# A fused attention and spectral-mixing kernel: two more quad loads, the last two modes by column halves, identity passes moved

## The chip, the cores and the metric

The kernel runs on one core of a Trainium2 chip. The metric is device time in microseconds (us) of one execution. The runs of the kernel before took 427.29, 425.5 and 425.84 us; the median is 425.84 us. One further execution was profiled: it took 425.88 us.

## The reference

Two stages are chained. The first is a sparse causal attention on 8 batches, 8 heads, 576 positions and head size 64. Heads 0 to 3 see the last 32 positions ("local"), heads 4 to 7 see every 32nd earlier position ("strided"). The second takes the heads side by side as `x` (8 x 576 x 512) and mixes it in the frequency domain:

```python
X = np.fft.rfft(x, axis=1)
Xr, Xi = (np.real(X[:, :n_modes]), np.imag(X[:, :n_modes]))
Yr = np.einsum('bmd,mde->bme', Xr, w_r) - np.einsum('bmd,mde->bme', Xi, w_i)
Yi = np.einsum('bmd,mde->bme', Xr, w_i) + np.einsum('bmd,mde->bme', Xi, w_r)
Y[:, :n_modes] = Yr + 1j * Yi
y = np.fft.irfft(Y, n=S, axis=1)
u = x + y
return (u + np.maximum(u @ w_ch, 0.0)).astype(np.float32)
```

There are 64 modes, and each has its own pair of 512 x 512 weights. In float32 these are 134 MB of the inputs, while q, k and v are 9.4 MB each and the output is 9.4 MB.

## The kernel before, in words

All loads that change float32 to float16 are issued by GpSimd (POOL), in program order: q, k, v by batch, then the mode weights. The weights are taken in "halves": half 1 holds input rows 256 to 511 of each mode and half 0 holds rows 0 to 255. `ORDER` lists (half, mode): modes 0 to 55 of half 1, 0 to 47 of half 0, then the 8 last of half 1 and the 16 last of half 0. Two consecutive entries are a "pair". A pair is loaded by two DMAs, one of `moe_w_r` into partitions 0 to 63 and one of `moe_w_i` into partitions 64 to 127, of 512 KB (float16) each. At the pair numbers in `QUADS` two pairs are loaded together by two DMAs of 1024 KB.

`w_fetch` (the function that issues at lines 187 to 194) is called after each consumed pair. It counts a free pair and issues while there is room: a pair needs one free pair, a quad needs two, and it returns without issuing when there are fewer. The weights live in `wring`, a ring of five pairs; pairs 1, 2 and 7 are guests in other buffers, and consuming them frees nothing. Eight pairs (0 to 7) are issued during the strided attention. The local attention of batch b then runs on TensorE (PE) in a hand-written order, mixed with `NMODES[b]` modes, 14 for batch 0, so pairs 0 to 6 are consumed in batch 0. `load_loc(6)` is issued just before them and `load_loc(7)` at the start of batch 1. All waits between engines follow from which tiles the instructions touch. Where a matmul and another engine use one PSUM bank, they take turns even on different columns.

After half 1's 56 and half 0's 48 modes, 24 modes remain (`rest`, line 1073). Half 0 is computed one mode at a time by `mode` (lines 619 to 652): 4 column blocks `e` of 128, 4 contraction steps each, 16 matmuls (L634) into one PSUM bank that holds eight modes. VectorE (DVE) then adds the half-1 part from PSUM and writes the spectrum `YT` (`spectrum`, L567): once for modes 56 to 61, once for 62 and 63. Between the modes `late[i]` inserts other work: `renew` updates `x` and `x @ w_ch` by the first 48 modes (L966, L769, L971), and after mode 62 it starts output items 0 and 1: `v_early(0)`, `v_early(1)`, `u_early(0)`. These are identity matmuls of 128 x 512 that copy `x @ w_ch` (L997) or `x` (L1007) into PSUM.

When mode 63 is done, `spec_z(3, 0)` (L745) multiplies batches 0 to 3 of the last spectrum by `w_ch`; ScalarE (ACT) copies it to `zzs[0]`; eight transposes (L1076) give the spectrum itself, copied by DVE (L1078) to `yys`. These two tiles lie in a PSUM pool of their own, opened when the pool of the modes is closed.

The output has 18 items, each of two 128 x 512 blocks. An item needs `v_early` and `new_rows` on `zzs` (L1018) in one PSUM pair, a relu by ACT (L1041, float32), `u_early` and `new_rows` on `yys` in another PSUM pair, a DVE add (L1055) and a store issued by SyncE (SP, L1058). `pieces(k)` says whether the add and the store go by whole item or by halves. `pooled(k, j)` says whether GpSimd adds `x` to the relu's result (L1044) in place of an identity matmul.

Of the kernel before, what the change touches and what calls it, by code (L numbers as in the profile page):

```python
# [10 lines left out]
FP = mybir.dt.float32  # L11
F16 = mybir.dt.float16
AluOp = mybir.AluOpType
ACTF = mybir.ActivationFunctionType
# [5 lines left out]
NM = 64  # L20
# [36 lines left out]
def kernel(  # L57
# [10 lines left out]
    nc = tc.nc  # L68
    PSUM = bass.MemoryType.PSUM
# [5 lines left out]
    pss = {}  # L75
# [10 lines left out]
    def psum(kind, half=False, pair=False):  # L86
        if pair:
            return pss[kind].tile([128, 2, 512], FP, tag=kind, name=kind)
        if half:
            return pss[kind].tile([128, 1024], F16, tag=kind, name=kind)  # L90
        return pss[kind].tile([128, 512], FP, tag=kind, name=kind)
# [19 lines left out]
    idn = cs["cI"]  # L111
# [8 lines left out]
    YS = {}  # L120
# [29 lines left out]
    ORDER = [(1, m) for m in range(SPLIT1)] + [(0, m) for m in range(SPLIT0)]  # L150
    ORDER += [(1, m) for m in range(SPLIT1, NM)] + [(0, m) for m in range(SPLIT0, NM)]
    UNEVEN = {64: (25, 12, 27), 84: (6, 54, 4), 94: (10, 54)}
    QUADS = {p for p in range(13, 54) if (p - 13) % 5 in (0, 2)}
    wring = pw.tile([128, 2 * NWBUF, 4, DM], F16, tag="w", bufs=1, name="wring")
    w_tiles = []
    w_chs = {}
# [4 lines left out]
    def w_fetch(n=1):  # L161
        free_pairs[0] += n
        while len(w_tiles) < 2 * NM:
            i = len(w_tiles)
            pair = i // 2
            nm = 4 if pair in QUADS else 2
            if 2 * free_pairs[0] < nm:
# [86 lines left out]
    def act_copy(out, in_):  # L254
        nc.scalar.activation(out=out, in_=in_, func=ACTF.Copy)  # L255
# [300 lines left out]
    ypt = {}  # L556
    queued = []

    def flush():
        while queued:  # L560
            queued.pop()()

    def spectrum(slot, part, src):
        if slot == 0:
            nc.scalar.activation(out=YS["Y0"][part], in_=src, func=ACTF.Copy)
        else:
            nc.vector.tensor_tensor(  # L567
                out=YS["YT"][part], in0=src, in1=YS["Y0"][part], op=AluOp.add
            )
# [19 lines left out]
    def mode_pair(slot, m):  # L589
        half = 1 - slot  # L590
        if m % 4 == 0:
            ypt[slot] = psum("y")
        yp = ypt[slot]
        steps = [(c, mm) for c in range(4) for mm in (m, m + 1)]
        if m == 0:
            steps.sort(key=lambda x: x[1])
        for c, mm in steps:
            wt = w_tiles[ORDER.index((half, mm))]
            pr = ds(0, 128 if mm else 64)
            a = 32 * (mm % 4)  # L600
            nc.tensor.matmul(  # L601
                yp[ds(a, 32), :],
                Xh[half][pr, c].rearrange("p b r (h m) -> p (b r h) m", h=2)[
                    :, :, mm % 32
                ],
                wt[pr, XC[c], :],
                start=(c == 0),
                stop=(c == 3),
                tile_position=(0, a),
            )  # L610
        if slot or m // 2 not in GUEST:
            w_fetch()
        if m % 4:
            yr = big.tile([128, DM], F16, tag="yr", name="yr")
            act_copy(yr, yp)
            queued.append(lambda: four_turned(slot, m - 2, yr))

    def mode(slot, m):
        half = 1 - slot
        if m % 2:  # L620
            flush()
        if slot == 0 or m < SPLIT0:
            if m % 2:
                mode_pair(slot, m - 1)
            return
        mi, mg = m % 8, m // 8
        if mi == 0:
            ypt[slot] = psum("y")
        yp = ypt[slot]
        yv = yp.rearrange("p (m e x) -> p m e x", m=8, e=4)  # L630
        wt = w_tiles[ORDER.index((half, m))]
        for e in range(4):
            for c in range(4):
                nc.tensor.matmul(  # L634
                    yv[:, mi, e, :],
                    wt[:, XC[c], ds(128 * e, 128)],
                    Xh[half][:, c, :, :, m],
                    start=(c == 0),
                    stop=(c == 3),
                )  # L640
        if m % 2:
            w_fetch()
        ends = {5: 6, 7: 2} if mg == 7 else {7: 8}
        if mi in ends:
            n = ends[mi]
            m0 = mi + 1 - n
            spectrum(
                slot,
                (slice(None), slice(None), mg // 2, slice(None), ds(8 * (mg % 2) + m0, n)),
                yp.rearrange("p (m e x) -> p e x m", m=8, e=4)[:, :, :, ds(m0, n)],  # L650
            )
# [90 lines left out]
    def spec_z(g, bq, zp):  # L742
        for e in range(4):
            lhs = YS["YT"][:, e, g, ds(8 * bq, 8), :].rearrange("p x m -> p (x m)")
            nc.tensor.matmul(  # L745
                zp, lhs, w_chs["n"][:, e, :], start=(e == 0), stop=(e == 3)
            )
# [102 lines left out]
    for b in range(B):  # L850
# [3 lines left out]
        ends = [lambda h=h: loc_scores(b, h, True) for h in (0, 2)]  # L854
# [23 lines left out]
    zzs = [ptr.tile([128, DM], F16, name=f"zz{i}") for i in range(B)]  # L878
    yys = [ptr.tile([128, DM], F16, name=f"yy{i}") for i in range(B)]
# [22 lines left out]
    for b in range(B + 1):  # L902
        for t in range(5):
            if b > 0 and (t < 4 or b % 2 == 0):
                work.append(lambda b=b, t=t: premix(b - 1, t))
            if b < B and t < 4:
                half, cp = ((1, 0), (1, 1), (0, 0), (0, 1))[t]
# [30 lines left out]
    for m in range(SPLIT0):  # L938
        mode(1, m)
        upto = -(-len(work) * (m + 1) // SPLIT0)  # L940
        for w in work[n:upto]:
            w()
        n = upto
        if m >= 16 and m % 16 in (2, 4):
            spec(m // 16 - 1, m % 16 // 2 - 1)
# [5 lines left out]
    def spec_late(mm, kept, eng):  # L951
        up = psum("p", pair=True)
        for bq in range(2):
            mm(2, bq, up[:, bq])
        for b in range(B):
            eng(kept[b][64:96], up[ds(32 * (b % 4), 32), b // 4])
# [19 lines left out]
    late = {0: [lambda: spec_late(spec_z, zzs, act_copy)], 1: [spec_last]}  # L976
    for n, i in enumerate([3, 5, 7] + list(range(8, 21))):
        b, t = n // 2, n % 2 * 2
# [9 lines left out]
    vps, ups, rls, osbs = {}, {}, {}, []  # L988

    def own(item, kept, half):  # L990
        bs, t = item
        return [kept[b][:, t] for b in bs] if t < 4 else [half[b // 2] for b in bs[::2]]

    def v_early(k):
        vps[k] = psum("p", pair=True)
        for j, r in enumerate(own(items[k], v0s, v0h)):
            nc.tensor.matmul(vps[k][:, j], idn, r, start=True, stop=False)  # L997

    def pooled(k, j):
        return j == 1 and k in (4, 5, 6)  # L1000

    def u_early(k):
        ups[k] = psum(("p", "u")[k % 2], pair=True)
        for j, r in enumerate(own(items[k], xos, xoh)):
            if pooled(k, j):
                continue
            nc.tensor.matmul(ups[k][:, j], idn, r, start=True, stop=False)  # L1007
# [23 lines left out]
        )  # L1031

    def pieces(k):
        return [slice(0, 1), slice(1, 2)] if k in (0, 4, 5, 6) else [slice(0, 2)]

    def v_done(k):
        rl = ptr.tile([128, 2, 576], FP, tag=("xT", "rl")[k // 2 % 2], bufs=2, name="rl")
        rls[k] = rl[:, :, 0:DM]
        vp = vps.pop(k)
        for j in [slice(0, 2)] if k else pieces(k):  # L1040
            nc.scalar.activation(out=rls[k][:, j], in_=vp[:, j], func=ACTF.Relu)  # L1041
        for j, r in enumerate(own(items[k], xos, xoh)):
            if pooled(k, j):
                nc.gpsimd.tensor_tensor(  # L1044
                    out=rls[k][:, j], in0=rls[k][:, j], in1=r, op=AluOp.add
                )
# [12 lines left out]

    flush()  # L1060
    rest = [(0, m) for m in range(SPLIT1, NM)] + [(1, m) for m in range(SPLIT0, NM)]
    late[22] = [lambda: v_early(0), lambda: v_early(1), lambda: u_early(0)]
    for i, (slot, m) in enumerate(rest):
        mode(slot, m)
        for w in late.get(i, ()):
            w()
    yctx.close()
    with tc.tile_pool(name="ps_s", bufs=1, space=PSUM) as pss["s"]:
        zp = pss["s"].tile([128, 512], FP, name="zp")
        yp = pss["s"].tile([128, 2, 512], F16, name="yp")  # L1070
        spec_z(3, 0, zp)
        act_copy(zzs[0], zp)
        for bq in range(2):
            for e in range(4):
                lhs = YS["YT"][:, e, 3, ds(8 * bq, 8), :].rearrange("p x m -> p (x m)")
                nc.tensor.transpose(yp[:, bq, ds(128 * e, 128)], lhs, idn)  # L1076
        for bq in range(2):
            nc.vector.tensor_copy(out=yys[bq], in_=yp[:, bq])  # L1078
    pss["u"] = pctx.enter_context(tc.tile_pool(name="ps_u", bufs=1, space=PSUM))

    for k in range(2):
# [1 line left out]
    for k in range(2):  # L1083
        v_done(k)
    for k in range(2):
        if k:
            u_early(k)
        new_rows(k, ups[k], yys)
        u_done(k)
    for k in range(2, LAST + 2):  # L1090
# [47 lines left out]
```

## Time and profile before

| | |
|---|---|
| median of the runs | 425.84 us |
| the profiled execution | 425.88 us, span 424.1 us |
| mean granted TensorE clock | 0.933 |
| busy time: PE, DVE, ACT, POOL | 340.9, 234.6, 219.0, 95.7 us |
| DMA of the loads' queue (software) | 81.28 MB, 96.7% of the 16 DMA engines' span |
| DMA of the stores' queue (hardware) | 9.65 MB, 6.2% |
| last landing of a weight DMA | 390.66 us (issued 380.53, 10.1 us earlier) |
| first store issued | 395.42 us |
| last store issued, landed | 419.08 us, 422.89 us |

Times inside the execution are microseconds from the start of the span. PEld is the weight load of TensorE. A row "idle before <-releaser" tells how long an engine stood still before a group and what ended that. DMA share is the mean busy share of the 16 DMA engines; it reads up to 1.1 where they are never idle, since the records of their packets overlap a little.

### The profile page before, as it was taken

What the parts mean: (1) busy time and instruction counts of PE and PEld (TensorE: products, weight loads), DVE (VectorE), ACT (ScalarE), POOL (GpSimd) and SP (SyncE); (2) the same over time, 40 slices, a digit from 0 to 9 for tenths busy, and PEclk for the clock granted to TensorE, in tenths of its full rate; (3) what the DMA queues carried; (4) which work ended last, traced back from release to release, by engine and by line L of the source; (5) the groups of instructions that cost most, each with busy time, mean ns of one, the idle gap of its engine ahead of it and who ended that gap; (6) DMA issues with size and microseconds to landing.
All of it is one profiled execution on the core that took longest, in us unless ns stands there. A gap on an engine that the chain in (4) does not pass through costs nothing.

```text
span 424.1 us, 9718 instructions
## 1 busy us (share of the span) xinstructions
PE 340.9 (80%) x4164; PEld 206.5 (49%) x4164; DVE 234.6 (55%) x469; ACT 219.0 (52%) x391; POOL 95.7 (23%) x165
## 2 busy tenths in 40 slices
PE   2987878769999298889874959895779979989993
PEld 2866767554656155556542425453344534535331
DVE  3788788950354134545323326864385646555794
ACT  1687678642666056565753323622162365534772
POOL 7332333322422011102122101212111232310200
PEclk9999899967999789999998789999798998989999
DMA  8999999999999999999999999999999999997598
GB/s 147 211 212 213 213 212 214 210 212 210 214 214 211 215 216 213 214 215 214 211 215 213 212 211 216 213 213 214 213 214 211 214 214 214 213 213 145 196 380 316
DMA packets 30347, 91.62 MB, mean 216 GB/s; under 512 B 3873, under 2 KB 4641, under 8 KB 30305
## 3 DMA queue, kind: packets, MB, share of 16 engines
q0 software_dynamic: 24624, 81.28, 96.7%
q1 hardware_dynamic: 5248, 9.65, 6.2%
q8 instruction: 32, 0.52, 0.5%
q10 hardware_dynamic: 432, 0.08, 0.1%
q14 instruction: 11, 0.08, 0.0%
HBM read 162.83 MB, written 9.44 MB: 406 GB/s over the span
## 4 chain that ended last, share of the span: by engine, by line
PE 46%; DMA 23%; DVE 17%; ACT 8%; issue 4%; POOL 1%; DVEq 0%; ACTq 0%; POOLq 0%
DMA wring<-in_moe_w_i_dram 22%; PE y L601 11%; PE sc L726 5%; DVE xb L245 3%; ACT X L255 3%; DVE kz L287 3%; DVE yy L761 2%; PE p L997 2%; PE tp L417 2%; PE y L536 2%; PE sc L536 2%; PE sc L463 2%; PE p L769 2%; PE p L1018 1%; ACT PL L493 1%
## 5 line engine op out<-in xcount | busy, mean ns | idle before, releaser
L601 PE MATMUL y<-wring,X 128*32 128x512 f16 (+1 forms) x424 | 65.8, 422 | 23.6 <-DMA wring<-in_moe_w_i_dram 23.6
L190 POOL DMA_DIRECT2D wring<-in_moe_w_r_dram x39 | 23.6, 606 | 204.3 <-PE y L601 180.6
L601 PEld LDWEIGHTS <-X 128*32 128x32 f16 (+1 forms) x448 | 27.5, 139 | 41.4 <-DMA wring<-in_moe_w_i_dram 24.3
L735 ACT ACTIVATE v<-sc 128x512 f16<-128x512 f32 x32 | 19.1, 597 | 45.4 <-PE sc L726 45.4
L736 DVE COPY xo<-tp 128x512 f16<-128x512 f16 x32 | 22.1, 691 | 36.5 <-PE tp L734 36.4
L255 ACT ACTIVATE yr<-y 128x512 f16<-128x512 f32 x28 | 16.7, 597 | 41.2 <-PE y L601 41.0
L726 PE MATMUL sc<-w_cp,xT 128*128 128x512 f16 x128 | 36.2, 404 | 1.9 <-DVE xT L694 1.9
L245 DVE TENSOR_TENSOR xb<-av,rec 90x256 f16<-90x256 f32 (+2 forms) x80 | 36.0, 450 | 2.8
L493 ACT ACTIVATE PL<-sc 128x480 f16<-128x480 f32 (+1 forms) x48 | 26.9, 578 | 20.1 <-PE sc L479 19.8
L244 DVE RECIPROCAL rec<-av 90x4 f32<-90x4 f32 (+2 forms) x80 | 14.6, 183 | 39.3 <-PE av L508 28.2
L424 DVE COPY qT<-tp 128x576 f16<-128x576 f16 x16 | 11.9, 752 | 38.1 <-PE tp L417 38.1
L971 DVE TENSOR_TENSOR xo<-p,xo 128x1024 f16<-128x1024 f32 x16 | 19.6, 1225 | 14.3 <-PE p L769 14.3
L190 POOL DMA_DIRECT2D wring<-in_moe_w_i_dram x42 | 25.6, 609 | 6.1 <-DMA ring<-in_k_dram 2.0
L382 ACT ACTIVATE PL<-sc 90x360 f16<-90x360 f32 (+1 forms) x48 | 22.7, 490 | 7.1 <-PE sc L375 6.6
L255 ACT ACTIVATE v<-p 128x1024 f16<-128x1024 f32 x16 | 16.4, 1024 | 17.4 <-PE p L769 17.4
L255 ACT ACTIVATE v<-tp 128x640 f16<-128x640 f16 (+1 forms) x24 | 19.0, 807 | 11.6 <-PE tp L451 9.3
L417 PE MATMUL tp<-cI_s,ring 64*64 64x64 f16 x864 | 22.2, 196 | 2.7 <-DVE qT L424 2.4
L463 PE MATMUL sc<-cMl_s,cI_s 128*128 128x480 f16 (+1 forms) x48 | 18.9, 395 | 5.1 <-ACT PL L493 3.5
L280 PE MATMUL tp<-cI_s,ring 72*128 72x72 f16 x256 | 15.4, 207 | 9.1 <-DMA ring<-in_v_dram 7.4
L255 ACT ACTIVATE kz<-tp 64x360 f16<-64x360 f16 (+1 forms) x32 | 18.9, 592 | 6.2 <-PE tp L417 5.2
L417 PEld LDWEIGHTS <-ring 64*64 64x64 f16 x864 | 17.3, 109 | 9.0 <-issue 4.9
L536 PEld LDWEIGHTS <-xb 108*128 108x128 f16 (+2 forms) x176 | 15.4, 106 | 11.7 <-DVE xb L245 7.6
(146 smaller groups left out, 747.9 us busy)
## 6 DMA issues: line engine op xcount, KB each, us to landing
wring<-in_moe_w_r_dram POOLq DMA_DIRECT2D x17, 1024.0 KB, 13.3
wring<-in_moe_w_i_dram POOLq DMA_DIRECT2D x16, 1024.0 KB, 17.5
wring<-in_moe_w_i_dram POOLq DMA_DIRECT2D x24, 512.0 KB, 15.1
wring<-in_moe_w_r_dram POOLq DMA_DIRECT2D x22, 512.0 KB, 13.4
out_dram<-osb SPq DMA_DIRECT2D x14, 512.0 KB, 3.8
ring<-in_v_dram POOLq DMA_DIRECT2D x8, 288.0 KB, 13.3
ring<-in_q_dram POOLq DMA_DIRECT2D x8, 288.0 KB, 13.5
ring<-in_k_dram POOLq DMA_DIRECT2D x8, 288.0 KB, 13.1
```

What stands on the lines that cost most here:

```text
L190: nc.gpsimd.dma_start(dst, rows)
L245: nc.vector.tensor_tensor(out=dst, in0=val.rearrange("p h (q c) -> p h c q", c=4), in1=rec[0:n, 0:pieces] .to_broadcast((n, pieces, 64)) . ...
L255: nc.scalar.activation(out=out, in_=in_, func=ACTF.Copy)
L382: nc.scalar.activation(out=PS[0:n, ds(POFF[t], 4 * n)], in_=scp[0:n, 0 : 4 * n], func=ACTF.Exp, scale=SCALE,)
L417: nc.tensor.transpose(tp[ds(64 * hp, 64), ds(64 * i, 64)], qn[ds(64 * hp, 64), ds(64 * (9 * g + i), 64)], idn[ds(64 * hp, 64), ds(64 * hp, ...
L463: nc.tensor.matmul(scp[:, 0 : n * times].rearrange("p (h x) -> p h x", h=times), idn, mask_rows("cMl", n, times), start=True, stop=False,)
L493: nc.scalar.activation(out=dst, in_=src, func=ACTF.Exp, scale=SCALE)
L536: nc.tensor.matmul(xp[:, ds(192 * cp, 192)].rearrange("p (f m) -> p f m", f=3), xb[b][0:n, base + t, ds(128 * cp, 128)], F[0:n, :, t, :], ...
L601: nc.tensor.matmul(yp[ds(a, 32), :], Xh[half][pr, c].rearrange("p b r (h m) -> p (b r h) m", h=2)[:, :, mm % 32], wt[pr, XC[c], :], start= ...
L726: nc.tensor.matmul(vp, xT[:, ch], w_chs["cp"][:, ch, :], start=(ch == 0), stop=(ch == 3),)
L736: nc.vector.tensor_copy(out=xo.rearrange("p (h q c) -> p h q c", h=2, c=4), in_=tp[:, 0:512].rearrange("p (h c q) -> p h q c", h=2, c=4),)
L971: nc.vector.tensor_tensor(out=xo, in0=up[:, 0:n], in1=xo, op=AluOp.add)
```

## The change

1. `QUADS` starts at pair 8 in place of 13. The old set is 13, 15, 18, 20, ... and the new one is 8, 10, 13, 15, 18, 20, ...: pairs 8 and 9 become one quad, and pairs 10 and 11 another.
2. Modes 62 and 63 write columns e = 0, 1 into one PSUM tile and e = 2, 3 into another. The spectrum of both modes is added by two DVE instructions, one after e = 1 and one after e = 3 of mode 63.
3. After mode 62 only `v_early(1)` is left. `v_early(0)` follows `spec_z(3, 0)` and precedes the transposes; `u_early(0)` moves into the loop over items 0 and 1. `zp` and `yp` come from the modes' own PSUM pool.
4. The relu of item 0 is one instruction in place of two halves.
5. The adds and stores of items 1 and 2 (the second and third) go by halves.
6. GpSimd adds `x` to the second half of item 2 also.

```diff
-    QUADS = {p for p in range(13, 54) if (p - 13) % 5 in (0, 2)}
+    QUADS = {p for p in range(8, 54) if (p - 8) % 5 in (0, 2)}
...
+        if m == NM - 2:
+            ypt["last"] = [psum("y") for _ in range(2)]
+        if m >= NM - 2:
+            yl = [y.rearrange("p (m e x) -> p m e x", m=8, e=4) for y in ypt["last"]]
         wt = w_tiles[ORDER.index((half, m))]
         for e in range(4):
+            if m >= NM - 2:
+                yv = yl[e // 2]
             for c in range(4):
...
+            if m == NM - 1 and e % 2:
+                es = slice(e - 1, e + 1)
+                spectrum(
+                    slot,
+                    (slice(None), es, mg // 2, slice(None), ds(14, 2)),
+                    yv[:, ds(6, 2), es].rearrange("p m e x -> p e x m"),
+                )
         if m % 2:
             w_fetch()
-        ends = {5: 6, 7: 2} if mg == 7 else {7: 8}
+        ends = {5: 6} if mg == 7 else {7: 8}
...
     def pooled(k, j):
-        return j == 1 and k in (4, 5, 6)
+        return j == 1 and k in (2, 4, 5, 6)
...
     def pieces(k):
-        return [slice(0, 1), slice(1, 2)] if k in (0, 4, 5, 6) else [slice(0, 2)]
+        return [slice(0, 1), slice(1, 2)] if k in (0, 1, 2, 4, 5, 6) else [slice(0, 2)]
...
-        for j in [slice(0, 2)] if k else pieces(k):
-            nc.scalar.activation(out=rls[k][:, j], in_=vp[:, j], func=ACTF.Relu)
+        nc.scalar.activation(out=rls[k], in_=vp, func=ACTF.Relu)
...
-    late[22] = [lambda: v_early(0), lambda: v_early(1), lambda: u_early(0)]
+    late[22] = [lambda: v_early(1)]
...
+    zp = psum("y")
+    yp = psum("y", half=True).rearrange("p (b x) -> p b x", b=2)
+    spec_z(3, 0, zp)
+    act_copy(zzs[0], zp)
+    v_early(0)
+    for bq in range(2):
+        for e in range(4):
+            lhs = YS["YT"][:, e, 3, ds(8 * bq, 8), :].rearrange("p x m -> p (x m)")
+            nc.tensor.transpose(yp[:, bq, ds(128 * e, 128)], lhs, idn)
+    for bq in range(2):
+        nc.vector.tensor_copy(out=yys[bq], in_=yp[:, bq])
     yctx.close()
...
     for k in range(2):
-        if k:
-            u_early(k)
+        u_early(k)
         new_rows(k, ups[k], yys)
         u_done(k)
```

## The prediction

> **What bounds the kernel now.** I read the page first, then the waits of GpSimd's queue, the landings of single DMAs, the last stage in order of time, and stretches of half a microsecond.
>
> ```profile
> DMA  8999999999999999999999999999999999997598
> q0 software_dynamic: 24624, 81.28, 96.7%
> PE 46%; DMA 23%; DVE 17%; ACT 8%; issue 4%; POOL 1%; DVEq 0%; ACTq 0%; POOLq 0%
> ```
>
> The DMA engines are busy from start to end but for one dip near slice 37. The records of the loads' queue show no gap over 0.05 us between its first packet (2.91) and its last (390.35). So the loads form one saturated stream, and whatever idles its engines moves its end. The chain names PE often, but it returns to the weights' DMAs (22% of the span).
>
> ```profile
> 97.90 0.54 POOL L233 DMA_DIRECT2D ring<-in_k_dram  x1 [0.86 <-DMA ring<-in_v_dram]
> 101.10 0.60 POOL L190 DMA_DIRECT2D wring<-in_moe_w_r_dram  x1 [2.66 <-PE y L601]
> 101.70 0.60 POOL L190 DMA_DIRECT2D wring<-in_moe_w_i_dram  x1
> 107.70 0.58 POOL L190 DMA_DIRECT2D wring<-in_moe_w_r_dram  x1 [5.40 <-PE y L601]
> 110.31 0.59 POOL L190 DMA_DIRECT2D wring<-in_moe_w_r_dram  x1 [1.44 <-PE y L601]
> 112.25 0.59 POOL L190 DMA_DIRECT2D wring<-in_moe_w_r_dram  x1 [0.77 <-PE y L601]
> ```
>
> These are pairs 8, 9, 10 and 11, each released by PE's last matmul of pair 0, 3, 4 and 5. Between 97.90 and 107.70 pair 8 is all that is issued.
>
> ```profile
> ring<-in_k_dram POOLq DMA_DIRECT2D x1, 288.0 KB, 11.0
> wring<-in_moe_w_r_dram POOLq DMA_DIRECT2D x1, 512.0 KB, 10.2
> wring<-in_moe_w_r_dram POOLq DMA_DIRECT2D x1, 1024.0 KB, 9.0
> ```
>
> Issue to landing of the DMAs of 97.90, 101.10 and 316.98: the last local load lands at 108.86, pair 8's first half 2.5 later, back to back.
>
> ```profile
> 389.08 0.64 PE L634 MATMUL y<-X,wring 128*128 128x16 f16 x16 [0.53 <-DVE YT L567]
> 390.85 0.64 PE L634 MATMUL y<-X,wring 128*128 128x16 f16 x16
> 391.52 0.29 DVE L567 TENSOR_TENSOR YT<-y,Y 128x128 f16<-128x128 f32 x1 [1.90 <-PE y L634]
> 391.87 1.04 PE L745 MATMUL zp<-w_ch,YT 128*128 128x512 f16 x4 [0.39 <-DVE YT L567]
> 392.99 0.60 ACT L255 ACTIVATE zz<-zp 128x512 f16<-128x512 f32 x1 [4.03 <-PE zp L745]
> 394.07 3.11 ACT L1041 ACTIVATE rl<-p 128x512 f32<-128x512 f32 x4 [0.48 <-PE p L1018]
> 394.70 1.29 DVE L1055 TENSOR_TENSOR osb<-p,rl 128x512 f32<-128x512 f32 x2 [0.55 <-ACT rl L1041]
> 395.42 24.03 SPq L1058 DMA_DIRECT2D out_dram<-osb  x22
> ```
>
> Mode 63's last DMA (issued 380.53, 10.1 to landing) lands at 390.66, and mode 63 starts at once: the landing releases it, not the identity passes ahead of it. From landing to first store 4.76 us pass.
>
> ```profile
> 96.00:99.00 3.00, 3.00 (x12) 1.15 (x10) 0.00 (x0) 1.14 (x2) 1.08 (x2) 0.50 1.12 211
> 388.00:388.50 0.50, 0.50 (x4) 0.11 (x5) 0.50 (x2) 0.13 (x1) 0.00 (x0) 1.00 0.76 148
> 389.00:389.50 0.50, 0.42 (x15) 0.42 (x15) 0.50 (x2) 0.00 (x0) 0.00 (x0) 1.00 0.43 82
> 397.50:398.00 0.50, 0.50 (x3) 0.21 (x3) 0.38 (x1) 0.49 (x1) 0.00 (x0) 1.00 0.32 115
> 399.50:400.00 0.50, 0.47 (x6) 0.24 (x6) 0.50 (x1) 0.44 (x2) 0.02 (x1) 1.00 0.24 86
> ```
>
> The last three columns are granted clock, DMA share, GB/s. The loads run dry engine by engine (0.76, then 0.43). The stores first starve, and from 400.5 on every half microsecond to 422 has a share near 1: then DMA bounds the output, whatever PE and DVE do.
>
> **Quads at 8 and 10.** The four DMAs at 101.10 to 108.27 become two of 1024 KB that need two free pairs, that is pair 3's matmuls: they issue at 107.70, not 101.10. The DMA records show when the 16 engines finish the last local load: between 105.66 and 108.86, mean 107.03. From an issue to work on an idle engine takes 1.7 us at the kernel's start (issue 1.23, first packet 2.91). At 316.98 the two earliest engines had run dry: they complete that 1024 KB at 324.40 and 324.55, and 4.95 us of transfer earlier is 319.45, 2.47 us after the issue. I take the latter, the same size in mid-run: work resumes at 110.2. The last engine loses 1.35 us, the first 4.5, the mean 3.15. The bytes left are equal for all engines, so the end moves by about the mean if their spread at the end is today's. Bounds: 1.35 and 4.5. I take 3.1.
>
> What the quads save: 512 KB land every 2.46 us (347 to 372) and 1024 KB every 4.90, so 0.02 us a pair, nothing. [...]
>
> On other queues: the second quad issues at 112.25 with pair 5 and has 7 us of work ahead of it; pair 12 and the local load of 116.49 follow in today's order. The second quad's last half lands near 110.2 + 4 x 4.9 = 129.8, and PE wants it at 128.27: 1.5 us of waiting, covered by PE's 8.16 us wait for the DMA that ends at 147.66. Without that cover it would cost 1.5.
>
> **Columns by halves, identity passes.** Mode 62's first tile no longer waits 0.53 us for DVE (its second takes the buffer that DVE still reads, and waits); but mode 63 waits for its landing, so this and the 0.86 us (4 x 0.215) of identity passes removed ahead of it gain at most 0.15. The first DVE half runs beside e = 2, 3; `spec_z` starts on e = 0, 1 about 0.4 earlier (the 0.39 idle goes), and so does ACT's copy. DVE pays one fixed start more: 0.29 becomes two of some 0.22 (128 columns 0.29, 384 columns 0.55), one of them covered. `v_early(0)` then takes 0.43 on PE ahead of the transposes, which stay where they are; `new_rows` starts 0.3 earlier, not 0.4. `u_early(0)`, 0.43, hides under the relu. If `spec_z` waited for both halves, the 0.4 is lost.
>
> **Relu whole, halves, GpSimd.** The first add waits 1.02 us for the relu in place of 0.59: +0.43. First store: -0.3 + 0.43 = +0.13. Items 1 and 2 in halves cost DVE 2 x 0.69 for 1.22, +0.15 each, but their stores start half an item earlier, where the stores starve: between 397.5 and 400.5 the shares (0.32, 0.44, 0.24, 0.64 where 1 is possible) leave 1.2 us idle, the most that can come back. GpSimd's add (3.38 us for three, 1.13 each) ends later than an identity pass of 0.215 and holds item 2's second half some 0.5 us; item 3's add waits on DVE behind it. SP issues two stores more, 0.37 each, under adds of 0.69. Tail: between -1.1 and +0.6; stepping the stores through at 0.685 us per 256 KB (383 GB/s) gives -0.4.
>
> **Sum.** +3.1 - 0.4 = +2.7 on the profiled execution's 425.88 (span 424.1 and 1.8 around it; 0.04 above the median): 428.6 us, +0.6%. Its own range is 427.6 to 430.0.
>
> **The rivals.** 0.5%, 2.1 us, is about what a measurement of this kernel tells from no change.
>
> *Pair 3 is freed sooner (not slower).* PE ran at half clock from 91.1 to 101.3 (0.50 above): 2.10, 1.7 and 3.76 us of matmuls that at full clock would take some 3.3 less. Released at 104.4, the quad would start at 106.9: a mean loss of 0.3, and 425.8. From an issue before 103.2 (105.66 less 2.47) nothing is lost. Against it: PE waited 1.7 us before 91 and again before 95, with the same work after the change. [...]
>
> *Only the last engine counts:* 1.35 - 0.4, 426.8. For it: it is last today by 0.1. Against: mean work is conserved, and the spread at the end (mean 0.79 before the last at 387.64) can't absorb 1.8.
>
> *The engines that were first come out last:* 4.5 - 0.4, 430.0. The loads of 221 to 291 in uneven pieces shift work between engines, for a spread that the bubble removes.
>
> *Faster:* no bubble and the whole 1.1 of the tail, 424.8. If the stream also paid each DMA's issue (0.60 on GpSimd), four fewer would bring 2.4 more: 422.4. The equal spacings speak against it.
>
> **How the numbers follow.** Forecast 0.58, freed sooner 0.17, last engine 0.12, first come last 0.08, faster 0.05. Slower by over 0.5%: 0.54 of the forecast's and 0.08, 0.62. Faster 0.05 less what stays within, 0.04; within 0.34. The range 425.7 to 430.2 takes in all bounds and leaves out about 0.1 on top and the faster case below.
>
> **What would show it.** GpSimd with no issue from 97.90 to about 107.7, then two quads; DMA share well below 1 between 106 and 110.5; last weight landing near 393.8; PE waiting at pair 10; landing to first store still near 4.9; fewer starved stretches after the first store. No dip at 106 to 110 would prove me wrong, as would an issue by 103.

## The result, and the profile after

The changed kernel takes 430.40 us (median of six executions, 429.07 to 433.82) against 425.82 us for the kernel before beside it. The ratio is 1.0115, 95% interval 1.0073 to 1.0158: slower. The forecast of 428.6 had the direction; the time lies 0.2 us above its range. The profiled execution took 429.93 us, with a span of 428.2 (424.1 before).

The same lines as before, first from the page of the changed kernel:

```profile
DMA  8999999999999999999999999999999999996498
q0 software_dynamic: 24560, 81.28, 96.3%
DMA 32%; PE 31%; DVE 8%; ACT 4%; issue 2%; POOL 1%; DVEq 0%; ACTq 0%; POOLq 0%
```

The bytes are those of before, their share of the span is smaller, and the chain that ended last now goes through the DMAs for 32% of the span (23% before). The dip near slice 37 is a little deeper. Forty slices of 10.7 us hide the other place, which GpSimd's timeline shows:

```profile
97.90 0.54 POOL L233 DMA_DIRECT2D ring<-in_k_dram  x1 [0.86 <-DMA ring<-in_v_dram]
106.54 0.63 POOL L190 DMA_DIRECT2D wring<-in_moe_w_r_dram  x1 [8.10 <-PE y L601]
107.16 0.63 POOL L190 DMA_DIRECT2D wring<-in_moe_w_i_dram  x1
111.10 0.61 POOL L190 DMA_DIRECT2D wring<-in_moe_w_r_dram  x1 [3.31 <-PE y L601]
```

GpSimd waits 8.10 us for PE before the first quad, where the kernel before issued pair 8 at 101.10. The stretches of one microsecond around it (last three columns: granted clock, DMA share, GB/s):

```profile
106.00:107.00 1.00, 1.00 (x27) 0.67 (x23) 0.25 (x1) 0.60 (x1) 0.46 (x1) 1.00 0.55 104
107.00:108.00 1.00, 0.99 (x28) 0.79 (x26) 0.91 (x2) 0.72 (x2) 0.79 (x2) 1.00 0.31 40
108.00:109.00 1.00, 1.00 (x15) 0.49 (x12) 0.35 (x1) 0.26 (x1) 0.00 (x0) 1.00 0.98 139
```

The loads run dry for about two microseconds, 106 to 108; a dip was forecast, between 106 and 110.5. The last weight lands at 393.65 in place of 390.66, +2.98 (forecast +3.1), and PE waits 2.97 us at pair 10 (the matmuls at 130.65). That costs nothing of its own: PE's next long wait for a DMA, which ends at 149.60 in place of 147.66, shrinks to 6.23 us from 8.16. The lines, two of the changed kernel and then one of the kernel before:

```profile
130.65 1.82 PE L601 MATMUL y<-wring,X 128*32 128x512 f16 x8 [2.97 <-DMA wring<-in_moe_w_i_dram]
149.60 1.92 PE L601 MATMUL y<-wring,X 128*32 128x512 f16 x8 [6.23 <-DMA wring<-in_moe_w_i_dram]
```

```profile
147.66 1.92 PE L601 MATMUL y<-wring,X 128*32 128x512 f16 x8 [8.16 <-DMA wring<-in_moe_w_i_dram]
```

What was not forecast is in the timeline of the last stage:

```profile
391.31 0.64 PE L640 MATMUL y<-X,wring 128*128 128x16 f16 x16 [0.97 <-DMA wring<-in_moe_w_i_dram]
391.78 0.59 PE L1010 MATMUL p<-v,cI_s 128*128 128x512 f16 x2
393.78 0.64 PE L640 MATMUL y<-X,wring 128*128 128x16 f16 x16 [1.41 <-DMA wring<-in_moe_w_i_dram]
394.22 0.47 DVE L567 TENSOR_TENSOR YT<-y,Y 128x64 f16<-128x64 f32 x2 [2.81 <-PE y L640]
394.50 1.89 PE L758 MATMUL y<-w_ch,YT 128*128 128x512 f16 x4
396.18 1.05 PE L1010 MATMUL p<-v,cI_s 128*128 128x512 f16 x2
396.43 0.60 ACT L255 ACTIVATE zz<-y 128x512 f16<-128x512 f32 x1 [5.67 <-PE y L758]
397.61 0.39 PE L1031 MATMUL p<-zz,cFl_s 32*128 32x512 f16 x4
399.09 1.29 DVE L1067 TENSOR_TENSOR osb<-p,rl 128x512 f32<-128x512 f32 x2 [0.62 <-ACT rl L1053]
399.81 4.21 SPq L1070 DMA_DIRECT2D out_dram<-osb  x6
```

From the last landing to the first store 6.16 us pass, against 4.76 before and the 4.9 forecast. `spec_z` (L758) takes 1.89 us for the same four matmuls that took 1.04, and `v_early(0)` (the L1010 at 396.18) 1.05 us, where two such matmuls took 0.59 at 391.78. The clock says why. Here are three stretches of 3.41 us of the changed kernel, with bounds where the records of its clock change (the first number behind the comma is PE's busy time, the third from the end the granted clock):

```profile
386.84:390.26 3.42, 3.42 (x46) 1.87 (x43) 2.37 (x3) 2.15 (x3) 0.00 (x0) 1.00 1.07 213
390.26:393.67 3.41, 1.14 (x20) 0.60 (x18) 1.14 (x3) 0.50 (x1) 0.00 (x0) 1.00 0.45 89
393.67:397.08 3.41, 3.22 (x23) 1.49 (x24) 0.45 (x2) 0.60 (x1) 0.00 (x0) 0.50 0.00 0
```

and the same places of the kernel before, with bounds set in the same way:

```profile
388.06:391.48 3.42, 2.89 (x42) 1.68 (x39) 1.56 (x3) 0.60 (x1) 0.00 (x0) 1.00 0.26 49
391.48:394.89 3.41, 2.74 (x23) 1.33 (x22) 1.24 (x4) 1.42 (x3) 0.00 (x0) 1.00 0.00 0
```

In the stretch that holds the last landing, PE is busy for 2.89 of 3.42 us before and for 1.14 of 3.41 after. Of the 1.75 us between them the moved passes are 0.86; mode 63, 0.64, lies inside this stretch before and behind its end after. The next stretch has the full clock before and half of it after, and this stretch holds the chain of mode 63, `spec_z` and the transposes. From the first store to the last landing 27.25 us pass, against 27.47. The parts make up the difference of the spans: 2.98 + 1.40 - 0.22 = 4.16, for 4.1 (428.2 less 424.1).

### The profile page after: what moved, and what is told of

The parts are those of the page before. It is cut to its first block, busy times and chain, and to the rows that moved or that the text cites. A ratio compares the mean times of both kernels' runs of the same rounds, so it can differ in the third digit from the quotient of the medians.

```text
span 428.2 us, 9719 instructions
## 1 busy us (share of the span) xinstructions
PE 342.0 (80%) x4163; PEld 206.0 (48%) x4163; DVE 235.1 (55%) x472; ACT 219.1 (51%) x390; POOL 94.6 (22%) x162
## 4 chain that ended last, share of the span: by engine, by line
DMA 32%; PE 31%; DVE 8%; ACT 4%; issue 2%; POOL 1%; DVEq 0%; ACTq 0%; POOLq 0%
DMA wring<-in_moe_w_i_dram 31%; PE y L601 9%; PE sc L739 5%; DVE yy L774 2%; PE y L536 2%; ACT X L255 2%; PE tp L417 2%; PE sc L463 2%; ACT PL L493 1%; PE tp L747 1%; PE p L1010 1%; PE sc L479 1%; DVE osb L1067 1%; DVE xb L245 1%; PE p L1031 1%
## 5 line engine op out<-in xcount | busy, mean ns | idle before, releaser
L601 PE MATMUL y<-wring,X 128*32 128x512 f16 (+1 forms) x424 | 66.7, 427 | 24.3 <-DMA wring<-in_moe_w_i_dram 24.2
L190 POOL DMA_DIRECT2D wring<-in_moe_w_r_dram x37 | 22.5, 608 | 211.9 <-PE y L601 190.2
L190 POOL DMA_DIRECT2D wring<-in_moe_w_i_dram x40 | 24.3, 609 | 7.7 <-DMA wring<-in_moe_w_i_dram 3.5
L1053 ACT ACTIVATE rl<-p 128x1024 f32<-128x1024 f32 x18 | 18.3, 1024 | 6.0 <-PE p L1031 4.1
```

Of the source, the lines that this page charges most:

```text
L190: nc.gpsimd.dma_start(dst, rows)
L601: nc.tensor.matmul(yp[ds(a, 32), :], Xh[half][pr, c].rearrange("p b r (h m) -> p (b r h) m", h=2)[:, :, mm % 32], wt[pr, XC[c], :], start= ...
```

## The experiments

Two theories were put against their rivals. **A, the gap:** the quad at pair 8 empties the loads' queue, and this alone is the quads' cost. **B, the clock:** the passes that were moved away had kept PE busy between modes 62 and 63; without them the clock falls to half just ahead of the last chain. Each kernel was timed beside the kernel before on one chip; times are medians, ratios stand with their 95% intervals. Names that begin with q_ or b_ are the kernel before with one part of the change, names that begin with a_ are the changed kernel, as it is or with parts undone or a filler added. Each kernel has one trace; landings, clocks and stretches are those of that one execution.

### The quads alone

```diff
-    QUADS = {p for p in range(13, 54) if (p - 13) % 5 in (0, 2)}
+    QUADS = {p for p in range(8, 54) if (p - 8) % 5 in (0, 2)}               # q_both
+    QUADS = {p for p in range(13, 54) if (p - 13) % 5 in (0, 2)} | {8}       # q_8
+    QUADS = {p for p in range(13, 54) if (p - 13) % 5 in (0, 2)} | {9}       # q_9
+    QUADS = {p for p in range(13, 54) if (p - 13) % 5 in (0, 2)} | {10}      # q_10
```

> The kernel before with the new set of quads alone (pairs 8 and 10 by quads, as in the changed kernel). The tail is the old one. Theory A, the bubble: GpSimd issues nothing between 97.9 and about 106.5 to 107.7, the DMA share falls below 0.6 for 1 to 2 us after 106, and the last weight lands some 3 us later than before's 390.66, so near 393.6; the time is about 3 us above before, ratio 1.006 to 1.0085. If the tail keeps its clock, landing to first store stays near 4.8 us; if the quads alone also bring the clock down in the last chain, it is near 6.1 and the ratio 1.010. Rival, the quads cost nothing and the whole loss is the tail's: ratio 0.999 to 1.001 and the last landing near 390.7.

> The kernel before with one quad more, at pair 8 (pairs 8 and 9 in two DMAs of 1024 KB, released with pair 3's matmuls); pair 10 on as before. Theory A: this quad alone empties the queue, since only the last local load lies ahead of it; the same gap as with both, about +3 us, ratio 1.006 to 1.0085. If the bubble came from both quads in equal parts it would be +1.5, ratio 1.0035.

> The kernel before with one quad more, at pair 9 (pairs 9 and 10 in two DMAs of 1024 KB); pair 8 is issued on its own near 101 as before. Theory A: pair 8's 1024 KB are 4.9 us of work, so the queue runs until 110.6 to 113.8 by engine; the quad is issued with pair 4 near 110.3 and work resumes about 2.4 later, at 112.7: the first engines lose up to 2.1 us, the last nothing, on the mean about 1; ratio 1.001 to 1.004. Rival, any larger DMA there costs its fixed part once: the same +3 us as with the quad at 8, ratio 1.007.

> The kernel before with one quad more, at pair 10 (pairs 10 and 11 in two DMAs of 1024 KB, released with pair 5's matmuls near 112.3). Theory A: pairs 8 and 9 lie ahead of it, about 9.8 us of work after 107, so nothing runs dry: ratio 0.999 to 1.001, PE waits up to 1.5 us at pair 10 and makes it up at its next long wait for a DMA. Rival, a quad costs by holding its data back from PE: +1.5 us, ratio 1.0035.

| kernel | time | before | ratio |
|---|---|---|---|
| q_both | 429.85 | 425.80 | 1.0100 (1.0078 to 1.0123) |
| q_8 | 428.99 | 425.80 | 1.0077 (1.0052 to 1.0101) |
| q_9 | 426.78 | 425.80 | 1.0031 (1.0008 to 1.0054) |
| q_10 | 426.08 | 425.80 | 1.0002 (0.9988 to 1.0017) |

The quad at 8 costs 3.19 us by itself, the quad at 10 nothing that can be told from zero, and one at 9, with pair 8 ahead of it as cover, about 1. That is theory A's order, and q_8, q_9 and q_10 lie in its ranges; in these runs a quad's cost went with what was left in the queue when it was issued, not with being a quad. The DMA share was 0.01 in the microsecond in which q_8's was issued (108 to 109) and 0.88 in that of q_9's (110 to 111); in q_10, whose quad was issued at 110.73, it was 1.01 or more in every microsecond from 104 to 115. q_both, 1.0100, lies above its range of 1.006 to 1.0085, and its last weight lands at 395.99, 5.33 us later than before, where 3 were expected: the gap alone doesn't make that up (see below). q_8's timeline and stretches of one microsecond show the gap at its widest:

```profile
108.06 0.62 POOL L190 DMA_DIRECT2D wring<-in_moe_w_r_dram  x1 [9.89 <-PE y L601]
```

```profile
107.00:108.00 1.00, 1.00 (x26) 0.54 (x22) 0.10 (x1) 0.49 (x2) 0.00 (x0) 1.00 0.15 28
108.00:109.00 1.00, 1.00 (x34) 0.72 (x27) 0.73 (x1) 0.75 (x2) 0.94 (x2) 1.00 0.01 2
109.00:110.00 1.00, 0.99 (x18) 0.70 (x12) 0.79 (x2) 0.70 (x2) 0.31 (x1) 1.00 0.73 82
```

and q_9's show no more than a nick:

```profile
110.00:111.00 1.00, 1.00 (x23) 0.87 (x21) 0.79 (x3) 0.54 (x1) 0.93 (x2) 1.00 0.88 176
112.00:113.00 1.00, 1.00 (x12) 0.59 (x9) 0.00 (x0) 1.00 (x2) 0.99 (x2) 1.00 0.97 160
```

In both of these kernels landing to first store stays at 4.6 us, and in q_both at 4.70, with a granted clock of 1.00 in all three from 387 to 401: here the quads by themselves didn't bring the clock down at the end.

### The passes back, a filler, and the change without its quads

In `a_idn` the passes return to their old place. In `a_fill` they stay moved, and the pass that is left is issued four times:

```diff
-    late[22] = [lambda: v_early(1)]
+    late[22] = [lambda: v_early(0), lambda: v_early(1), lambda: u_early(0)]  # a_idn; the later v_early(0), u_early(0) go
+    late[22] = [lambda: v_early(1, 4)]                                       # a_fill: times=4
...
+            for t in range(times):
+                nc.tensor.matmul(vps[k][:, j], idn, r, start=True, stop=t < times - 1)
```

`a_rep` is the changed kernel again, and `a_q13` is the changed kernel with the old `QUADS`.

> The changed kernel once more, as it is, for a second trace beside the next three. Theory B, the clock: with only 0.43 us of identity passes between modes 62 and 63, PE idles while it waits for the last two landings, and the clock falls to half for 3.41 us in the last chain; then landing to first store is again near 6.1 us (4.76 before). Rival: the drop was one execution's chance; then it is 4.5 to 4.9 us here. The time by both: 429.5 to 430.5, ratio 1.009 to 1.012, of which the gap at 106 to 110 makes 2.1 to 3.5 us by the moment at which pair 3 is done.

> The changed kernel with the identity passes put back where they were: v_early(0), v_early(1) and u_early(0), 1.29 us, between modes 62 and 63. Theory B: PE is busy again while it waits for the last landing, the clock stays at full, landing to first store 4.4 to 4.9 us, and the time is 0.5 to 1.4 us below the changed kernel's on the same chip (ratio to before 1.006 to 1.009). Rival, the place of the passes doesn't matter: same time as the changed kernel, within 0.3 us.

> The changed kernel with the one moved-to pass group kept busy on purpose: v_early(1) between modes 62 and 63 is issued four times over (the first three results are overwritten by the same product, so the output is unchanged), 1.72 us of PE work in place of 0.43, in time that PE spends idle for the last landing. v_early(0) and u_early(0) stay where the change put them. Theory B: extra work that computes nothing new makes the kernel faster: clock full in the last chain, landing to first store 4.5 to 4.9 us, 0.5 to 1.4 us below the changed kernel. Rival, the order of the passes and not the clock made the difference: no gain, or 0.2 us lost.

> The changed kernel with the old set of quads (13, 15, 18, ...): all parts of the change but the quads at 8 and 10. Theory A: no gap at 106 to 110, last weight landing near before's 390.7. The time then shows the tail alone: with theory B's clock drop 425.8 plus 0.5 to 1.2, ratio 1.001 to 1.003; without the drop 425.3 to 425.8, ratio 0.999 to 1.000. By the prediction's sum (tail -0.4) 425.4.

| kernel | time | before | ratio | last landing | landing to first store |
|---|---|---|---|---|---|
| a_rep | 430.19 | 426.46 | 1.0093 (1.0070 to 1.0115) | 393.79 | 6.51 |
| a_idn | 429.71 | 426.46 | 1.0099 (1.0065 to 1.0132) | 395.59 | 4.78 |
| a_fill | 429.61 | 426.46 | 1.0094 (1.0066 to 1.0122) | 393.66 | 4.91 |
| a_q13 | 427.90 | 426.46 | 1.0034 (1.0011 to 1.0056) | 389.80 | 6.11 |

In the traces theory B holds four times out of four: at half clock (0.50 from 394.98 to 398.39 in `a_rep`, from 389.72 to 393.14 in `a_q13`) the last chain takes 6.1 to 6.5 us, and with the passes back or the filler, where the clock stays at 1.00, 4.8 to 4.9. `a_q13` shows that the tail alone loses 1.44 us where the prediction had it gain 0.4. (Expected for `a_q13` with the clock's fall was a loss of 0.5 to 1.2.) But in time `a_idn` and `a_fill` are only 0.5 to 0.6 us below `a_rep`, by the ratios not at all, and the intervals overlap: the quads' gap was a different one in each of the three traces. The profiled one of `a_idn` issued its quad at 109.06, that of `a_rep` at 106.41. So these two don't settle theory B by time.

### One part alone, and a version meant to beat both

`b_move` is the kernel before with the passes moved, nothing else; `b_tail` is the kernel before with parts 4, 5 and 6 of the change; `a_q13_idn` is the changed kernel with old quads and the passes back; `best1` is `a_q13_idn` with two further lines as in the kernel before:

```diff
-    late[22] = [lambda: v_early(0), lambda: v_early(1), lambda: u_early(0)]
+    late[22] = [lambda: v_early(1)]          # b_move; v_early(0) after spec_z, u_early(k) for k = 0 too
...
-        return j == 1 and k in (2, 4, 5, 6)
+        return j == 1 and k in (4, 5, 6)     # best1
-        nc.scalar.activation(out=rls[k], in_=vp, func=ACTF.Relu)
+        for j in [slice(0, 2)] if k else pieces(k):
+            nc.scalar.activation(out=rls[k][:, j], in_=vp[:, j], func=ACTF.Relu)
```

> The kernel before with one part alone: of the 1.29 us of identity passes between modes 62 and 63 only v_early(1), 0.43 us, stays; v_early(0) comes behind spec_z and u_early(0) behind the first relu, as in the change. Old quads, whole columns, old stores. Theory B: this alone idles PE ahead of the last landing and brings the clock down; landing to first store from 4.7 to 6.1 or more, time 1.3 to 1.7 us above before, ratio 1.003 to 1.004. Rival, the drop needs the column halves or the later loads as well: then only v_early(0)'s 0.43 ahead of the transposes shows, ratio 1.000 to 1.001.

> The kernel before with the first relu whole, the adds and stores of items 2 and 3 in halves, and GpSimd's add for the third item; nothing else of the change. By the prediction: landing to first store +0.43 (5.1 to 5.2 us), first store to last landing 0.5 shorter; ratio 0.999 to 1.000. By the stores seen in the runs so far (27.3 us with the new code as with the old, starved time 0.9 to 1.0 us against 1.2): only -0.2 there, so +0.2 in all, ratio 1.000 to 1.001.

> The changed kernel with the old quads and with the passes put back between modes 62 and 63: what is left of the change are the column halves, the whole relu, and the halves and GpSimd's add at the items. Theories A and B together: no gap at 106 to 110, full clock in the last chain, landing to first store 4.6 to 4.9 us; the 1.44 us that the kernel with the old quads alone lost against before go back to 0 to 0.2; ratio 0.999 to 1.001. Rival, the old quads' version lost for another reason than the clock: ratio 1.003 again.

> A version meant to beat both: the kernel before with the column halves of mode 63 and the items 2 and 3 in halves; the passes stay between modes 62 and 63, the first relu stays in two pieces, GpSimd adds for items 5 to 7 only, quads as before. Theory: landing to first store 4.2 to 4.4 us (-0.35 for the column halves), stores 0 to 0.3 shorter without the wait for GpSimd; 0.4 to 0.7 us below before, ratio 0.9985 to 0.999. Rival, the last mode's halves gain nothing against the landing: ratio 1.000.

| kernel | time | before | ratio | landing to first store |
|---|---|---|---|---|
| b_move | 427.66 | 426.11 | 1.0031 (1.0014 to 1.0048) | 7.29 |
| b_tail | 426.49 | 426.11 | 1.0007 (0.9990 to 1.0023) | 5.13 |
| a_q13_idn | 425.63 | 426.11 | 0.9990 (0.9971 to 1.0009) | 4.77 |
| best1 | 425.46 | 426.11 | 0.9978 (0.9962 to 0.9994) | 4.35 |

`b_move` is the plainest: a move of two of the three groups of matmuls, and nothing else, costs 1.55 us. Two of its stretches of 3.41 us:

```profile
386.02:389.43 3.41, 2.26 (x37) 1.08 (x33) 2.26 (x3) 1.16 (x2) 0.00 (x0) 1.00 0.82 162
389.43:392.84 3.41, 1.97 (x20) 1.07 (x21) 0.29 (x1) 0.00 (x0) 0.00 (x0) 0.50 0.02 4
```

Half clock begins 0.9 us ahead of the last landing (390.35) here and lasts for two stretches, to 396.26, so the chain took 7.29 us. `b_tail` shows the relu's price as forecast, 5.13 for 4.75 us (+0.38, forecast +0.43). Its time is not told from that of the kernel before, so no gain from the halves shows either. In `best1` the relu is in halves again and the column halves stay:

```profile
390.76 0.64 PE L640 MATMUL y<-X,wring 128*128 128x16 f16 x16 [0.62 <-DMA wring<-in_moe_w_i_dram]
391.19 0.46 DVE L567 TENSOR_TENSOR YT<-y,Y 128x64 f16<-128x64 f32 x2 [2.48 <-PE y L640]
391.47 1.04 PE L758 MATMUL y<-w_ch,YT 128*128 128x512 f16 x4
393.20 0.40 PE L1031 MATMUL p<-zz,cFl_s 32*128 32x512 f16 x4 [0.24 <-ACT zz L255]
394.25 1.29 DVE L1068 TENSOR_TENSOR osb<-p,rl 128x512 f32<-128x512 f32 x2 [0.50 <-ACT rl L1054]
```

and `new_rows` of the kernel before, where mode 63 started at 390.85:

```profile
393.64 0.40 PE L1018 MATMUL p<-zz,cFl_s 32*128 32x512 f16 x4 [0.29 <-ACT zz L255]
```

`spec_z` starts 0.71 us after mode 63 (1.02 before) and `new_rows` (L1031) 2.44 after (2.79 before): the column halves are worth 0.35 us while the clock holds.

### The clock or the order

Still open was whether the clock alone makes up the loss in time, or the order of the passes. Without the quads at 8 and 10 their scatter is gone. `a_q13_rep` is `a_q13` again; `a_q13_fill` adds the filler of `a_fill`, and no pass changes its place.

> The changed kernel with the old quads once more, as the base of the next run. Theory B: the clock falls to half again in the last chain, landing to first store 6.0 to 6.6 us, time 1.0 to 1.8 us above before, ratio 1.0025 to 1.004. Rival, the drop was chance: ratio 1.000 to 1.001.

> The same with v_early(1) issued four times over between modes 62 and 63 (the first three results are overwritten by the same product; the output is unchanged), and every pass in the place that the change gave it. Theory B, the clock alone: landing to first store 4.8 to 5.0 us, the time falls by 1.2 to 1.6 us against a_q13_rep, ratio to before 0.999 to 1.001. Rival, the order of the passes holds the loss: ratio 1.003 as without the filler.

> The version meant to beat both once more. Theory: landing to first store near 4.35 us as in its first trace, 0.4 to 0.8 us below before, ratio 0.998 to 0.999. Rival, its first result was the scatter of the executions: ratio 1.000.

| kernel | time | before | ratio | landing to first store |
|---|---|---|---|---|
| a_q13_rep | 427.30 | 426.29 | 1.0023 (1.0007 to 1.0040) | 7.31 |
| a_q13_fill | 426.04 | 426.29 | 0.9993 (0.9979 to 1.0008) | 4.91 |
| best1_rep | 425.66 | 426.29 | 0.9990 (0.9971 to 1.0010) | 4.35 |

Three groups of matmuls that compute nothing new take 1.26 us off the time, inside the 1.2 to 1.6 that theory B gave. Ten of the twelve executions without the filler took more than 426.5 us, two of the twelve with it, though the two intervals against the kernel before just touch. It is the clock, not the order. (The chain of `a_q13_rep`, 7.31 us, is longer than the 6.0 to 6.6 expected, because its clock stays at half for two stretches, 390.20 to 397.03.) The stretches of `a_q13_rep`:

```profile
386.79:390.20 3.41, 1.77 (x23) 0.76 (x22) 1.77 (x3) 0.67 (x2) 0.00 (x0) 1.00 0.55 108
390.20:393.62 3.42, 2.96 (x22) 1.44 (x23) 0.45 (x2) 0.40 (x1) 0.00 (x0) 0.50 0.00 0
```

and of `a_q13_fill`, with the lines of its timeline for the filler, mode 63 and `spec_z` below:

```profile
386.68:390.10 3.42, 2.81 (x28) 1.17 (x24) 1.51 (x3) 0.60 (x1) 0.00 (x0) 1.00 0.60 119
390.10:393.51 3.41, 3.19 (x36) 1.79 (x36) 1.05 (x4) 0.87 (x2) 0.00 (x0) 1.00 0.00 0
```

```profile
388.17 1.89 PE L1011 MATMUL p<-v,cI_s 128*128 128x512 f16 x8
390.24 0.64 PE L640 MATMUL y<-X,wring 128*128 128x16 f16 x16 [0.19 <-DMA wring<-in_moe_w_i_dram]
390.96 1.04 PE L758 MATMUL y<-w_ch,YT 128*128 128x512 f16 x4
```

PE waits 0.19 us for the landing in place of 1.48, mode 63 starts no later, and `spec_z` is back at 1.04 us. `best1` came out 0.63 us below the kernel before again (0.65 the first time); the first interval excludes no change, the second does not.

## Why the prediction was right and wrong

**The quads: right in mechanism, and in size where the gap itself is concerned.** The prediction's formula was the issue plus 2.47 us, less the mean of the engines' ends of the last local load, 107.03; it put in today's 107.70 for the issue. Six traces have a quad at 8. The DMA records give, for each number of bytes loaded, how much later it was reached than in the kernel before; the gap is that lag's growth from 104 to 112 us.

| kernel | quad's issue | formula | gap | last landing |
|---|---|---|---|---|
| a_rep | 106.41 | 1.85 | 2.21 | +3.13 |
| the changed kernel | 106.54 | 1.98 | 2.15 | +2.98 |
| a_fill | 106.98 | 2.42 | 2.59 | +3.00 |
| q_both | 107.46 | 2.90 | 2.75 | +5.33 |
| q_8 | 108.06 | 3.50 | 3.44 | +4.76 |
| a_idn | 109.06 | 4.50 | 4.65 | +4.93 |

The gap follows the formula within 0.4 us. So the mean engine counts: for the changed kernel's landing of 108.83, "only the last engine" would have given 106.54 + 2.47 - 108.83 = 0.2 us. Of the rival that pair 3 is freed sooner one part is true: the release moves between 106.4 and 109.1 from one execution to another, and in these six traces PE has half clock until 100.1 to 103.1 us, with the release 4.8 to 6.4 after that; that the one sets the other is not shown. It never came by 103, where the gap would be gone. No cost for PE's wait at pair 10: right. No gain from fewer DMAs: right, by q_10 (1.0002).

What the step left out is that the loads fall behind by another 0.4 to 2.5 us after the gap. The +2.98 of the changed kernel is a gap of 2.15 and 0.8 more, so its agreement with +3.1 is partly luck. In q_both about 1 us of it falls near 290, where packets took 0.41 us on the mean for 4 us and 0.31 in the kernel before; the stretch from 286.35 to 289.76 moved 177 GB/s, and the kernel before 213 there. In the nine other traces without a quad at 8 or 9 the lag changed by -0.6 to +0.2 us from 112 to the end. What makes the rest is not settled. In medians the quads cost 3.19 (q_8) and 4.05 us (q_both) in the kernel before, but 2.29 in the changed one (a_rep against a_q13).

**Columns by halves, identity passes: the step that failed.** The step said that removing 0.86 us of passes ahead of mode 63 gains at most 0.15, since the landing releases mode 63. The landing does release it; but the step took PE's idle time there as free and put nothing down for the clock of the chain that follows. What the passes did was to hold PE's busy time up in the stretch ahead of the last chain (2.89 of 3.42 us before, 1.14 of 3.41 after). The first-store term, forecast +0.13, came out at +1.40 in the profiled execution and at +1.35 to +2.55 in the four other traces with the passes moved and no filler (a_rep, a_q13, b_move, a_q13_rep), because the clock was at half (0.50) in every one. None of the twelve traces with the passes in place or with the filler had that. With the filler the whole tail comes to -0.25 us in time (a_q13_fill, 0.9979 to 1.0008), which both the forecast -0.4 and no change fit. The parts that the step did price are right where the clock holds: the column halves 0.35 us (forecast 0.4), and landing to first store 4.91 us in both fillers (forecast 4.9).

**Relu whole: right.** +0.38 (b_tail against before) and +0.42 (4.77 in a_q13_idn against 4.35 in best1), forecast +0.43.

**Halves and GpSimd's add: no gain, where -0.5 was taken** (the tail's -0.4 less the +0.13 of its first store). From first store to last landing the old code took 27.01 to 27.51 us (mean 27.29 of six traces), the new one 26.74 to 27.72 (mean 27.27 of nine). Stores start half an item earlier: the third is issued 1.20 us after the first in the changed kernel, 1.94 before. The last store lands no sooner for it. One candidate is that item 2's second half waits for GpSimd. DVE's and GpSimd's timelines of the changed kernel:

```profile
402.97 0.69 DVE L1067 TENSOR_TENSOR osb<-p,rl 128x512 f32<-128x512 f32 x1 [0.47 <-POOL rl L1056]
```

```profile
401.78 1.16 POOL L1056 TENSOR_TENSOR rl<-rl,xo 128x512 f32<-128x512 f32 x1 [17.55 <-ACT rl L1053]
```

That half microsecond of waiting was in the text of the prediction. But it isn't shown to be the cause: in `best1` and `best1_rep` item 2 has no add on GpSimd and DVE no such wait there, and first store to last landing takes 27.02 and 27.82 us all the same. What gives the gain back stays open.

**The sum.** In the profiled execution the three parts above come to 4.16 us where 2.7 was forecast: the last landing is 0.1 better than forecast, the first store's term 1.27 worse and the stores 0.3 worse. The clock's fall is most of the miss. Among the runs, against the forecast's +3.1 - 0.4, the parts measured alone are +4.05 (q_both) and +1.44 or +1.01 (a_q13, twice). Their sum, 5.1 to 5.5, is more than the +4.58 and +3.73 of the changed kernel. The gap's scatter between the six traces, 2.2 to 4.7, is larger than the difference.

## What to carry to other kernels

Before idle-time work on PE is called free to move, look at the stretch that follows it: if a serial chain of matmuls comes next, that work may be what holds the chain's clock, as it did here (`spec_z` 1.04 us with the passes in place, 1.89 in the changed kernel). When it has to go, other work may take its place, as 1.89 us of filler did in `a_q13_fill`. Here a larger DMA that needed a later release held the loads back by at least what the queue ran short by at its issue, on the mean over the DMA engines (a gap of 2.15 to 4.65 us, and a last landing 2.98 to 5.33 us later, with a quad at 8), and by nothing that can be told from zero where the queue was full (q_10, 1.0002); ask how many microseconds of work lie ahead of it.

## What was not expected

How little waiting went with the fall. The granted clock of the kernel before and of the changed kernel changes at times that are whole steps of 3.41 us apart; 388.06 is one of them in the one and 390.26 in the other. In stretches laid on such times of each trace, PE was busy for 1.14 us (the changed kernel), 1.22 (`a_q13`), 1.77 (`a_q13_rep`), 1.93 (`a_rep`) and 2.26 (`b_move`) of the 3.41 just ahead of the half clock. In the twelve other traces every stretch that begins between 384 and 398 has a clock of 1.00, and the least busy of them in each trace has 2.21 (`q_both`) to 2.81 us (`a_q13_fill`). Busy time alone doesn't part the two: in `q_both`, with the passes in place, the stretch from 395.58 had 2.21 us of it and the full clock stayed, while `b_move` lost it after 2.26. Nor did PE stand still for long: in `a_rep` its longest wait between 391.57 and 394.98, ahead of the half clock, was 1.40 us.

```profile
391.57:394.98 3.41, 1.93 (x36) 1.22 (x35) 0.76 (x3) 0.00 (x0) 0.00 (x0) 1.00 0.20 40
394.98:398.39 3.41, 3.41 (x18) 1.51 (x15) 0.41 (x2) 0.60 (x1) 0.00 (x0) 0.50 0.00 0
```
